# Whole attention products and an uneven second layer in a fused attention and feed-forward kernel

## The chip, the cores and the metric

The kernel runs on one core of one Trainium2 chip. The core has a matrix engine (TensorE, PE in the profile, with its weight loads shown apart as PEld), a vector engine (VectorE, DVE), an activation engine (ScalarE, ACT), GpSimd (POOL) and SyncE (SP), which issues transfers here. Matrix results go to PSUM, an accumulator memory that the kernel divides into eight banks of 512 float32 columns on 128 partitions. The metric is the device time of one execution in microseconds (us); lower is better. Times of a single instruction are in nanoseconds (ns) where marked.

## The reference

The input is a batch of 8 with 8 heads, 576 tokens and 64 features for each head. Attention keeps only scores within `tau` of the row's maximum; its output, with the heads side by side, is the input of a two-layer block with a hard-swish gate.

```python
def _attn_ref(q, k, v, tau):                       # (8, 8, 576, 64)
    scale = 1.0 / np.sqrt(q.shape[-1])
    scores = scale * np.matmul(q, k.transpose(0, 1, 3, 2))
    thresh = np.max(scores, axis=-1, keepdims=True) - tau
    scores = np.where(scores >= thresh, scores, -1000000000.0)
    scores = scores - np.max(scores, axis=-1, keepdims=True)
    attn = np.exp(scores)
    attn = attn / (np.sum(attn, axis=-1, keepdims=True) + 1e-09)
    return np.matmul(attn, v).astype(np.float32)

def _moe_ref(x, w_in, w_out):                      # x (4608, 512)
    h = x @ w_in                                   # first layer, 512 -> 2048
    relu6 = np.clip(h + 3.0, 0.0, 6.0)
    g = h * relu6 / 6.0
    return (g @ w_out).astype(np.float32)          # second layer, 2048 -> 512
```

## The kernel before

Four heads of one batch are a quad; there are 16. A quad has nine slots: slots 0 to 3 are the four blocks of 128 queries of the first pair of heads, 4 to 7 those of the second pair, and slot 8 holds the last 64 queries of all four heads. The main loop runs over all 144 slots, `n`. From slot `N1 = 22` on it works in periods of two slots: scores of two slots are computed together at the end of an odd slot.

In each slot the loop weaves together softmax work for some slots, a piece of the first layer (`mm1`, eight matmuls of 256 columns or four of 512), attention products of a quad that is done (`multiply`), and, in even slots, half an output tile of the second layer (`second`, 8 of its 16 matmuls). The order of the statements is the order of the instructions on each engine.

```python
HB, OB = 6, 7                        # PSUM banks of the first and second layer

def bank():                          # banks 2 and 5 in turn: products, transposed last keys
    nonlocal turn
    turn += 1
    return ps[:, (2, 5)[turn % 2], :]

def first(n):
    return n > N1 + 2 and n % 2

def score_col(n, a):                 # scores of odd slots end inside banks 2 and 5
    return (704 if first(n) else 128) + (0 if a else 1536)

def scores(n):
    quad, slot = divmod(n, NSLOT)
    w0 = 320 if first(n) else 384
    for k0, w in ((0, w0), (w0, S - w0)):
        ...                          # two heads side by side, float32, 64 rows each
```

An attention product takes 128 probabilities by 64 values at a time. The two heads of a pair lie in the two halves of the output's partitions. `av_main` does the 512 queries of a pair (or part of them, by `c0` and `w`), `av_rest` the last 64 of four heads:

```python
def av(pb, pair, pT, cols):
    b, hp = divmod(pair, NPAIR)
    vm, vr = vsb[b]
    for c in range(4):
        for a in range(2):
            nc.tensor.matmul(pb[a * 64:(a + 1) * 64, :], vm[:, 2 * hp + a, c * D:(c + 1) * D],
                             pT[:, 5 * a + c, cols], start=(c == 0), stop=False)
    for a in range(2):
        nc.tensor.matmul(pb[a * 64:(a + 1) * 64, :], vr[:, a, hp, :], pT[:, 4, cols], start=False, stop=True)

def av_main(pair, c0=0, w=512):
    ...
    pb = bank()[:, 0:w]
    av(pb, pair, pts[pair], slice(c0, c0 + w))
    return lambda: nc.vector.tensor_copy(out=xT[b][:, hp, c0:c0 + w], in_=pb)
```

Which product follows which slot (counted from the quad's first) is in a table. In quads 2 to 15 each pair is done in two halves of 256 queries, in every second slot:

```python
if quad < NB:                        # NB = 2
    jobs = ((8, p0, 0, 512), (12, p1, 0, 512), (13, None, 0, 0))
else:
    jobs = [(7 - quad % 2 + 2 * i, *of) for i, of in enumerate(
        ((p0, 0, 256), (p0, 256, 256), (p1, 0, 256), (p1, 256, 256), (None, 0, 0)))]
```

The part of the loop that sets the order (cut):

```python
        if n + 1 < len(queue):
            sm_max(queue[n + 1])              # VectorE: scores out of PSUM, with the row's maximum
        even = n >= N1 and n % 2 == 0
        if n > N1:
            sm_recip(prev)
        for copy in waiting:                  # output of a second-layer tile, query transposes
            copy()
        waiting = []
        if todo1:
            item, then = todo1.pop(0)
            ...
            h = mm1(item, 0 if n == len(queue) - 1 else OB if n > N1 and n % 2 and not pieces else HB)
        if n >= N1:
            for copy in multiply(n):          # products, and their copies out of PSUM (VectorE)
                copy()
        if item:
            mm1_gate(item, h, mm1_relu(h, on_act=even))   # ReLU: ScalarE in even slots, else VectorE
        ...
            second()                          # 8 second-layer matmuls, in even slots
        if n >= N1:
            for i in range(2):
                sm_exp(sl, i)                 # ScalarE
            if n + 1 < len(queue):
                for i in range(2):
                    sm_mask(queue[n + 1], i)  # ScalarE
        ...                                   # transposes of later queries and keys
        elif n % 2:
            for m in (n + 3, n + 2):          # the even slot's scores first
                if m < len(queue):
                    scores(m)
        if n > 0:
            sm_norm(prev)                     # GpSimd, then a transposing transfer
```

Of the kernel before, what the change touches and what calls it, by code (L numbers as in the profile page):

```python
# [15 lines left out]
P = 128  # L16
# [4 lines left out]
def kernel(  # L21
# [11 lines left out]
    B, H, S, D = q.shape  # L33
# [4 lines left out]
    NI = d_ff // P  # L38
# [320 lines left out]
    def av_rest(quad):  # L359
        b, g = divmod(quad, 2)  # L360
        pb = bank()
        for n in range(2):
            av(pb[:, n * 64:(n + 1) * 64], 2 * quad + n, ptr[quad], slice(n * 64, (n + 1) * 64))
        if b % 2 == 0 and g == 0:
            xR[b // 2] = x_pool.tile([P, KI, P], BF16, tag="xR", name="xR")
        o0 = 64 * (b % 2)
        return lambda: nc.vector.tensor_copy(out=xR[b // 2][:, 2 * g:2 * g + 2, o0:o0 + 64],
                                             in_=pb[:, 0:P].rearrange("p (a b) -> p a b", a=2))
# [42 lines left out]
    def mm2_part(bb, mt, part, ob=OB):  # L411
        if part == 0:
            o_ps[0] = ps[:, ob, :]
        for ni in range(part * 4, part * 4 + 4):
            nc.tensor.matmul(o_ps[0], gbuf[:, ni, mt * P:(mt + 1) * P], w_out_sb[:, ni, :],  # L415
                             start=(ni == 0), stop=(ni == NI - 1))
# [23 lines left out]
    def moe_of(b):  # L440
        items = []
        for c0, mts in (((0, (5, 6)), (None, (4,)), (256, (7, 8))) if b % 2 else ((0, (0, 1)), (256, (2, 3)))):
            for ni in range(0, NI, 4 if c0 is None else 2):
                items.append(((b, ni, c0), ()))
            items[-1] = (items[-1][0], [(b // 2, mt, part) for mt in mts for part in range(4)])
# [41 lines left out]
    for quad in range(1, NQUAD):  # L487
        n0 = quad * NSLOT
        first_odd = n0 - 9 + quad % 2
        for i, (job, of) in enumerate((("q", 2 * quad), ("k", 2 * quad), ("rest", quad),  # L490
                                       ("q", 2 * quad + 1), ("k", 2 * quad + 1))):
            turn_at(n0 + (-5, -4, -3, 0, 1)[i] if quad < 3 else
                    first_odd + (0, 2, 3, 4, 6)[i] if quad > 3 else first_odd + (0, 2, 3, 5, 7)[i], job, of)

    products = {}
    for quad in range(NQUAD):
        p0, p1 = 2 * quad, 2 * quad + 1
        if quad < NB:
            jobs = ((8, p0, 0, 512), (12, p1, 0, 512), (13, None, 0, 0))
        else:  # L500
            jobs = [(7 - quad % 2 + 2 * i, *of) for i, of in enumerate(
                ((p0, 0, 256), (p0, 256, 256), (p1, 0, 256), (p1, 256, 256), (None, 0, 0)))]
# [3 lines left out]
    def multiply(n):  # L506
        copies = []
        for of, pair, *columns in products.get(n, ()):
            copies.append(av_rest(of) if pair is None else av_main(pair, *columns))
# [5 lines left out]

    def second():
        nonlocal pieces, bb, mt, part
        pieces = 2 if now % 2 == 0 and todo2 else 0
        for _ in range(pieces):
            bb, mt, part = todo2.pop(0)  # L520
            mm2_part(bb, mt, part)
# [3 lines left out]
    pieces = bb = mt = part = 0  # L525
    waiting = []
    for n, sl in enumerate(queue):
# [23 lines left out]
        for copy in waiting:  # L551
            copy()
        waiting = []

        if todo1:
# [3 lines left out]
            h = mm1(item, 0 if n == len(queue) - 1 else OB if n > N1 and n % 2 and not pieces else HB)  # L559
# [3 lines left out]
        if n >= N1:  # L563
            for copy in multiply(n):
                copy()
        if item:
            mm1_gate(item, h, mm1_relu(h, on_act=even))
        copies = pe_transpose(queue[n - 2]) if n > 1 and queue[n - 2].on_chip else None
# [20 lines left out]
        if part == 3:  # L589
            waiting.append(lambda tile=(bb, mt): late.extend(mm2_out(*tile, on_act=False)))  # L590
            part = 0
# [37 lines left out]
    count = [1, 0 if todo2 and todo2[0][2] else 1]  # L629
# [16 lines left out]
    def rest2():  # L646
        while todo2:
            bb, mt, part = todo2.pop(0)
            mm2_part(bb, mt, part, ob=OB - count[1] % 2)
            if part == 3:  # L650
                flush()
                if (bb, mt) == (B // 2 - 1, 8):
                    last_out()
                else:
                    late.extend(mm2_out(bb, mt, on_act=(count[1] % 2 == 0)))
                count[1] += 1

    av_main(2 * last + 1, 0, 256)()
    for item in todo1:
        rest1(*item, on_act=False)  # L660
# [48 lines left out]
```

## Time and profile before

| what | value |
|---|---|
| time, median of three runs | 520.26 us (520.13 to 520.81) |
| span of the profiled execution | 518.3 us |
| granted clock of TensorE, mean | 0.999 |
| costliest TensorE lines, busy | scores L287 174.0 us, second layer L415 134.1 us, first layer L381 130.9 us, products L346 39.1 us |
| costliest VectorE line | maximum L302, 205.1 us |
| costliest ScalarE lines | mask L309 205.8 us, exponential L314 192.5 us |

The profile's page gives for each engine the busy time, its share of the span and the number of instructions. Groups of instructions carry the line of the kernel, the engine, the operation, the tiles (output, arrow, inputs), the count, and then the busy time and the mean time of one. The timeline merges neighbouring instructions of one kind: start in us from the span's beginning, time from the first start to the last end, engine, line, operation, and in brackets how long the engine had been idle and what ended that. The ends of matmuls are modelled; the time from the start of one group to the start of the next is the measure of TensorE's work. The chain of waits follows the execution back from its last instruction, at each step to what released it.

### The profile page before, as it was taken

How to read it: one execution, taken by the hardware profiler on the slowest of the kernel's cores; microseconds unless marked ns; L12 is line 12 of the kernel's file. 1: busy time of each engine (PE TensorE's matmuls, PEld its weight loads, DVE VectorE, ACT ScalarE, POOL GpSimd, SP SyncE). 2: the span in 40 equal slices, each digit the busy share in tenths (PEclk: the TensorE clock that was granted, in tenths of full speed). 3: DMA queues.
4: the chain of work that ended last, by engine and by line, in shares of the span. 5: the costliest groups of instructions: out<-in, count | busy, mean ns of one | idle time of the engine just before them, and what ended most of it. 6: DMA issues, size and time to landing. Idle time of an engine off the chain costs nothing.

```text
span 518.3 us, 12124 instructions
## 1 busy us (share of the span) xinstructions
PE 505.9 (98%) x4145; PEld 321.1 (62%) x4145; DVE 442.6 (85%) x1124; ACT 452.1 (87%) x980; POOL 299.3 (58%) x538
## 2 busy tenths in 40 slices
PE   8999999999999999999999999999999999999997
PEld 6765556666665666666665666666665666667563
DVE  3788887998999999999999999999999999887261
ACT  3999979999999999999999999999999999987060
POOL 1778869756676666657566656657566655552000
PEclk9999999999999999999999999999999999999999
DMA  5899899989999999999979998999999997564222
GB/s 132 123 173 163 142 161 156 174 147 171 167 178 157 170 162 183 177 170 179 177 150 164 157 199 159 166 166 178 167 163 168 178 178 123 114 113 71 77 67 61
DMA packets 314094, 78.77 MB, mean 152 GB/s; under 512 B 296624, under 2 KB 309168, under 8 KB 314032
## 3 DMA queue, kind: packets, MB, share of 16 engines
q1 hardware_dynamic: 294464, 67.90, 76.0%
q0 software_dynamic: 18368, 9.71, 15.1%
q8 instruction: 32, 0.52, 0.4%
q10 hardware_dynamic: 1200, 0.39, 0.3%
q14 instruction: 30, 0.25, 0.2%
HBM read 36.70 MB, written 9.44 MB: 89 GB/s over the span
## 4 chain that ended last, share of the span: by engine, by line
PE 81%; ACT 3%; DVE 2%; POOL 0%; issue 0%; POOLq 0%
PE ps L287 25%; PE ps L415 24%; PE ps L381 21%; PE ps L346 7%; PE ps L376 3%; ACT s L314 1%; PE ps L349 1%; ACT s L309 1%; DVE g L404 1%; ACT r L389 1%; DVE s L302 0%; DVE r L391 0%; POOL pn L322 0%; PE ps L257 0%; ACT kT L222 0%; DVE xT L357 0%
## 5 line engine op out<-in xcount | busy, mean ns | idle before, releaser
L322 POOL TENSOR_SCALAR pn<-s,rinv 128x576 bf16<-128x576 f32 x288 | 210.6, 743 | 19.0 <-issue 4.5
L302 DVE TENSOR_SCALAR_CACHE_REDUCE s<-ps 128x576 f32<-128x576 f32 x288 | 205.1, 749 | 17.6 <-PE ps L287 9.0
L309 ACT ACTIVATE s<-s,bias 128x576 f32<-128x576 f32 x288 | 205.8, 763 | 6.0 <-POOL bias L305 5.7
L314 ACT ACTIVATE s<-s 128x576 f32<-128x576 f32 x288 | 192.5, 671 | 0.3
L287 PE MATMUL ps<-kT,qT 64*128 64x384 f32 (+7 forms) x1280 | 174.0, 419 | 4.7 <-DVE s L302 3.8
L287 PEld LDWEIGHTS ps<-kT,qT 64*128 64x128 f32 (+1 forms) x1280 | 103.6, 175 | 59.3 <-issue 15.8
L415 PE MATMUL ps<-w_out_sb,g 128*128 128x512 bf16 x576 | 134.1, 379 | 0.0
L381 PE MATMUL ps<-xT,w_in_sb 128*128 128x256 bf16 x1024 | 130.9, 273 | 0.2 <-DVE g L404 0.2
L381 PEld LDWEIGHTS <-w_in_sb 128*128 128x128 bf16 x1024 | 95.5, 98 | 40.0 <-issue 20.8
L305 POOL TENSOR_SCALAR bias<-m 128x2 f32<-128x2 f32 x144 | 26.9, 187 | 154.5 <-DVE rinv L317 136.6
L404 DVE SCALAR_TENSOR_TENSOR g<-r,ps 128x512 bf16<-128x512 f32 x128 | 87.9, 687 | 15.2 <-ACT r L389 11.2
L415 PEld LDWEIGHTS <-g 128*128 128x128 bf16 x576 | 56.2, 98 | 56.8 <-issue 0.4
L389 ACT ACTIVATE r<-ps,three 128x512 f32<-128x512 f32 x81 | 55.6, 687 | 27.9 <-PE ps L381 23.8
L314 ACT ACTIVATION_READ_ACCUMULATOR s<-s 128x1 f32 x288 | 54.5, 189 | 0.0
L391 DVE TENSOR_SCALAR r<-ps 128x512 f32<-128x512 f32 x63 | 42.9, 681 | 0.0
L346 PE MATMUL ps<-pT,vm 128*64 128x256 bf16 (+1 forms) x480 | 39.1, 285 | 0.0
L346 PEld LDWEIGHTS <-vm 128*64 128x64 bf16 x736 | 27.3, 110 | 16.0 <-issue 14.3
L357 DVE CAST xT<-ps 128x256 bf16<-128x256 f32 (+1 forms) x60 | 26.3, 438 | 11.8 <-PE ps L349 11.8
L423 DVE TENSOR_SCALAR osb<-ps 128x512 f32<-128x512 f32 x31 | 20.9, 673 | 8.4 <-PE ps L415 8.4
L302 DVE DVE_READ_ACCUMULATOR s<-ps 128x1 f32 x288 | 23.9, 83 | 0.0
L317 DVE RECIPROCAL rinv<-rsum 128x2 f32<-128x2 f32 x144 | 23.0, 160 | 0.6 <-ACT s L314 0.6
L143 POOL DMA_DIRECT2D vm<-in_v_dram x28 | 21.4, 765 | 0.7 <-issue 0.7
(57 smaller groups left out, 259.4 us busy)
## 6 DMA issues: line engine op xcount, KB each, us to landing
out_dram<-osb SPq DMA_DIRECT2D x31, 256.0 KB, 2.9
nq<-in_q_dram SPq DMA_DIRECT2D x96, 72.0 KB, 3.5
km<-in_k_dram SPq DMA_DIRECT2D x96, 64.0 KB, 3.2
vm<-in_v_dram POOLq DMA_DIRECT2D x24, 128.0 KB, 4.0
km<-in_k_dram SPq DMA_DIRECT2D x16, 128.0 KB, 3.6
w_in_sb<-in_moe_w_in_dram POOLq DMA_DIRECT2D x16, 128.0 KB, 3.6
w_out_sb<-in_moe_w_out_dram POOLq DMA_DIRECT2D x16, 128.0 KB, 4.1
pT<-pn SPq DMA_TRANSPOSE x117, 4.0
```

The source lines that it names most:

```text
L287: nc.tensor.matmul(ps_flat[rows, c0:c0 + w], qT_of(pair)[a * 64:(a + 1) * 64, q0:q0 + rows.stop - rows.start], kT_of(pair)[a * 64:(a + 1) ...
L302: nc.vector.tensor_scalar(out=sl.s[:, i, :], in0=ps_flat[:, c0:c0 + S], scalar1=1.0, scalar2=None, op0=Alu.mult, op1=Alu.max, accum_out=sl ...
L305: nc.gpsimd.tensor_scalar(out=sl.bias[:], in0=sl.m[:], scalar1=-scale, scalar2=tau, op0=Alu.mult, op1=Alu.add)
L309: nc.scalar.activation(out=s, in_=s, func=Act.Prelu, bias=sl.bias[:, i:i + 1], scale=scale, alpha=REJECT)
L314: nc.scalar.activation(out=s, in_=s, func=Act.Exp, accum_out=sl.rsum[:, i:i + 1])
L322: nc.gpsimd.tensor_scalar(out=pn[:, i, :], in0=sl.s[:, i, :], scalar1=sl.rinv[:, i:i + 1], scalar2=1.0, op0=Alu.mult, op1=Alu.mult)
L346: nc.tensor.matmul(pb[a * 64:(a + 1) * 64, :], vm[:, 2 * hp + a, c * D:(c + 1) * D], pT[:, 5 * a + c, cols], start=(c == 0), stop=False)
L381: nc.tensor.matmul(ps[:, hb, n * 256:(n + 1) * 256], w_in_sb[:, ki, (ni + n) * P:(ni + n + 1) * P], xT[b][:, ki, c0:c0 + 256], start=(ki = ...
L389: nc.scalar.activation(out=r, in_=hps, func=Act.Relu, bias=three[:])
L391: nc.vector.tensor_scalar(out=r, in0=hps, scalar1=3.0, scalar2=0.0, op0=Alu.add, op1=Alu.max)
L404: nc.vector.scalar_tensor_tensor(out=out, in0=r, scalar=6.0, in1=hps, op0=Alu.min, op1=Alu.mult)
L415: nc.tensor.matmul(o_ps[0], gbuf[:, ni, mt * P:(mt + 1) * P], w_out_sb[:, ni, :], start=(ni == 0), stop=(ni == NI - 1))
```

## The change

Most attention products of quads 2 to 15 are done whole, in 512 columns, where they were done in two halves; in quads 3, 7, 11 and 15 the second pair stays in halves. That makes the matmul work of products uneven among periods: some have 512 or more columns, some none. To even it out, the 16 second-layer matmuls of a token tile are no longer split 8 and 8 over the tile's two periods, but by the products near them: 5 and 11, 7 and 9 and so on. After a short part, the first-layer block of the odd slot goes to the bank of `bank()` that was used last (2 or 5) and not to `HB`, which the gate of the even slot may still read, and a product of the last 64 queries in that slot takes `HB`. The copies of products and the output of a second-layer tile stand behind the ReLU and the gate on VectorE, where they stood ahead. In even quads from 4 on, the transposition of the last keys (`"rest"`) comes two slots sooner. The product of the last 64 queries of a quad comes two slots sooner.

```diff
-    def av_rest(quad):
+    def av_rest(quad, pb=None):
         b, g = divmod(quad, 2)
-        pb = bank()
+        pb = bank() if pb is None else pb
...
-    def mm2_part(bb, mt, part, ob=OB):
-        if part == 0:
+    def mm2_part(bb, mt, n0, n1, ob=OB):
+        if n0 == 0:
             o_ps[0] = ps[:, ob, :]
-        for ni in range(part * 4, part * 4 + 4):
+        for ni in range(n0, n1):
...
-                    first_odd + (0, 2, 3, 4, 6)[i] if quad > 3 else first_odd + (0, 2, 3, 5, 7)[i], job, of)
+                    first_odd + (0, 2, 3 if quad % 2 else 1, 4, 6)[i] if quad > 3 else first_odd + (0, 2, 3, 5, 7)[i], job, of)
...
-            jobs = [(7 - quad % 2 + 2 * i, *of) for i, of in enumerate(
-                ((p0, 0, 256), (p0, 256, 256), (p1, 0, 256), (p1, 256, 256), (None, 0, 0)))]
+            jobs = (((9, p0, 0, 512), (13, p1, 0, 512), (13, None, 0, 0)) if quad % 2 == 0 else
+                    ((8, p0, 0, 512), (10, p1, 0, 256), (12, p1, 256, 256), (12, None, 0, 0)) if quad % 4 == 3 else
+                    ((8, p0, 0, 512), (12, p1, 0, 512), (12, None, 0, 0)))
...
-    def multiply(n):
+    def multiply(n, apart=False):
...
-            copies.append(av_rest(of) if pair is None else av_main(pair, *columns))
+            copies.append(av_rest(of, ps[:, HB, :] if apart else None) if pair is None else av_main(pair, *columns))
...
+    def columns_at(n):
+        return sum(of[3] or P for of in products.get(n, ()))
+
     def second():
-        nonlocal pieces, bb, mt, part
-        pieces = 2 if now % 2 == 0 and todo2 else 0
-        for _ in range(pieces):
-            bb, mt, part = todo2.pop(0)
-            mm2_part(bb, mt, part)
+        nonlocal pieces, done
+        pieces = 0
+        if now % 2 == 0 and todo2:
+            pieces = NI - done if done else NI // 2 + round((columns_at(now + 3) - columns_at(now + 1)) / 200)
+            mm2_part(*todo2[0], done, done + pieces)
+            done += pieces
...
-        for copy in waiting:
-            copy()
-        waiting = []
+        if n <= N1:
+            for copy in waiting:
+                copy()
+            waiting = []
...
-            h = mm1(item, 0 if n == len(queue) - 1 else OB if n > N1 and n % 2 and not pieces else HB)
+            apart = n > N1 and n % 2 and 0 < pieces < NI // 2
+            h = mm1(item, 0 if n == len(queue) - 1 else OB if n > N1 and n % 2 and not pieces else
+                    (2, 5)[turn % 2] if apart else HB)
...
-        if n >= N1:
-            for copy in multiply(n):
-                copy()
+        copies = multiply(n, item and apart) if n >= N1 else []
         if item:
             mm1_gate(item, h, mm1_relu(h, on_act=even))
+        if n >= N1:
+            for copy in copies + waiting:
+                copy()
+            waiting = []
```

Left out above is the bookkeeping of tiles and of the code behind the loop, which does the same work in the same order, except that it finds a tile with 9 of its 16 matmuls still to do (8 before) and one whole product in the place of a half.

## The prediction

> **What bounds the kernel now.** I read the page's first two parts, then the table of stretches, then the timeline and the chain of waits of one stretch in the middle. The page says which engine is full:
>
> ```profile
> PE 505.9 (98%) x4145; PEld 321.1 (62%) x4145; DVE 442.6 (85%) x1124; ACT 452.1 (87%) x980; POOL 299.3 (58%) x538
> ...
> 240.00:280.00 40.00, 40.00 (x330) 25.09 (x329) 38.14 (x99) 38.13 (x84) 24.14 (x44) 1.00 0.94 169
> ```
>
> 98% of TensorE (PE) alone proves little, since the ends of matmuls are modelled. In the second line, of the stretches, VectorE (DVE) and ScalarE (ACT) are also busy for 38.1 of 40 us: nearly as full. The timeline shows what paces them. One period is two slots; its TensorE part (start, duration of the group, line of the kernel):
>
> ```profile
> 260.37 0.63 PE L346 MATMUL ps<-pT,vm 128*64 128x256 bf16 x8
> 260.83 0.28 PE L349 MATMUL ps<-pT,vr 128*64 128x256 bf16 x2
> 261.04 2.21 PE L287 MATMUL ps<-kT,qT 64*128 64x384 f32 x16
> 263.18 1.05 PE L381 MATMUL ps<-xT,w_in_sb 128*128 128x256 bf16 x8
> 264.07 1.89 PE L415 MATMUL ps<-w_out_sb,g 128*128 128x512 bf16 x8
> 265.79 1.04 PE L381 MATMUL ps<-xT,w_in_sb 128*128 128x256 bf16 x8
> 266.76 0.63 PE L346 MATMUL ps<-pT,vm 128*64 128x256 bf16 x8
> 267.22 0.28 PE L349 MATMUL ps<-pT,vr 128*64 128x256 bf16 x2
> 267.43 2.21 PE L287 MATMUL ps<-kT,qT 64*128 64x384 f32 x16
> ```
>
> From start to start the costs are: scores 2.14, first layer 0.88 or 0.89, second layer 1.72 or 1.73 for eight matmuls, first layer 0.97, half an attention product 0.67; together 6.39 us, without a hole. The chain of waits for 254.4 to 280.3 names TensorE lines only. So TensorE sets the pace here, and its time from start to start is what counts. ScalarE and VectorE have this room in the same period:
>
> ```profile
> 264.27 0.69 ACT L389 ACTIVATE r<-ps,three 128x512 f32<-128x512 f32 x1 [0.31 <-PE ps L381]
> ...
> 261.15 0.42 DVE L357 CAST xT<-ps 128x256 bf16<-128x256 f32 x1 [0.36 <-PE ps L349]
> ...
> 264.99 0.69 DVE L404 SCALAR_TENSOR_TENSOR g<-r,ps 128x512 bf16<-128x512 f32 x1
> ...
> 266.94 0.16 DVE L317 RECIPROCAL rinv<-rsum 128x2 f32<-128x2 f32 x1
> 267.02 0.67 DVE L423 TENSOR_SCALAR osb<-ps 128x512 f32<-128x512 f32 x1
> ```
>
> ScalarE waits 0.3 us for the first layer, VectorE 0.36 us for the attention product. The second maximum ends at about 266.94, which is 5.90 after the scores began at 261.04, so VectorE releases the next scores about 0.4 us before TensorE comes for them. Before 105 us it is different: scores there take up to 2.9 us in the chain of waits, and the chain runs through ScalarE's masks and exponentials. I expect nothing from the change there.
>
> [...]
>
> **The change part by part.** The steady pattern repeats after four quads, 18 periods, 196.16 to 312.63 us by the scores' starts: 116.47 us.
>
> (1) Whole products. In 18 periods there are now 16 half products and four rests of 64 columns. Fourteen halves stand alone at 0.67 (9.38), two follow a rest (0.34 + 0.65 each, 1.98), two rests stand alone at 0.44 (0.88): 12.24 us. Afterwards there are seven whole products, two halves (the last pair of every fourth quad stays split) and four rests. A whole product was measured in the early stage at 1.20 from start to start; four alone are 4.80, three with a rest behind (1.20 + 0.33) 4.59, a half 0.67, a half with a rest 0.99: 11.05. Saved: 1.19 us, nearly all of it drains. Nine of 18 periods then have no product and go from first layer straight to scores; at 77.80 to 78.80 that step was 1.00, against 0.97 before a product, which gives 9 x 0.02 to 0.03, about 0.2, back.
>
> (2) The uneven split moves 3 of 16 second-layer matmuls, 3 x 0.216 = 0.65 us, from periods with a whole product into those without. It adds no work. Period with product: 2.14 + 0.88 + 5 x 0.216 + 0.97 + 1.20 = 6.27. Without: 2.14 + 0.88 + 11 x 0.216 + 0.99 = 6.39. With product and rest: 6.60. In two neighbours of every 18 no product is near either period of the tile, so the split is 8/8 and TensorE needs only 5.84 and 5.89.
>
> (3) The other bank for the first-layer block behind a short part removes a wait on the gate of the block before: in the four periods with a slot 8 the second layer took 1.82 before it instead of 1.73, up to 4 x 0.09 = 0.36 back.
>
> (4) The copies of products now stand behind ReLU and gate on VectorE. It no longer waits 0.36 for the product, and saves 7 x (838 - 690) = about 1 us in 18 periods, but the bank of the product comes free later.
>
> (5) Last keys of even quads, two slots sooner: the same 0.11 us on TensorE and the same two copies on ScalarE, moved to a period without product. No sum of its own.
>
> TensorE alone: -1.19 + 0.2 - 0.2 (half of the 0.36) = -1.2 of 116.47, 1.0%.
>
> **What it gives back.** VectorE's loop has a floor: scores 2.14, first layer 0.88, its end to ReLU 0.2, ReLU on ScalarE 0.7, gate 0.6, maximum 1.36, release 0.1: 6.0 us. The periods with 5.84 and 5.89 cannot be that short. The first follows the heaviest VectorE tail: maximum and reciprocal end at about 6.02, then ReLU 0.71, gate 0.60, copy 0.61, rest 0.20, output 0.59, key transpose 0.63 to 9.36, which is 2.76 into a period whose TensorE part before was 6.60. The maximum should start at 2.33, so all is 0.4 later, and the floor becomes 6.3; the second also holds the 24 score matmuls (2.30), floor 6.16. Lost: 0.48 + 0.27 = 0.75. And the copy of a whole product: reciprocal done at 5.98, + 0.71 + 0.60 + 0.69 = 7.98, or 1.71 into the next period, while the second half of the odd slot's scores wants that bank at 1.6. That is 0.1 to 0.15 in the three or four periods of 6.27 or 6.43: 0.3 to 0.5. Lost together 1.05 to 1.25. So the working leaves -0.1 to +0.1 in 18 periods, near nothing.
>
> **Rivals.** First, TensorE's saving arrives whole because VectorE's pieces overlap better than my steps: the freed wait of 0.36 in each product period speaks for it, VectorE's 95% share of the stretch against it. The steady part from 105.6 to 461.6 is 356 us, 3.06 patterns; x 1.2 = 3.7 us, so 516.6. Second, VectorE takes over as the pace: heavy periods sum to 4 x 0.67 + 0.16 + 0.60 + 1.31 + 0.61 + 0.20 + 0.59 + 0.69 = 6.84 against TensorE's 6.60. For it speaks the copy's late release; against it that the neighbours need only 5.3 and take up what is late. If each whole product stalls 0.4, 7 x 0.4 - 1.2 = +1.6 in 18 periods, 4.9 us, so 525. Third, ScalarE: in a period it does eight masks and exponentials at 0.66 from start to start and a ReLU of 0.58, 5.9 us, with the keys' copies (0.54) 6.44; in a period of 6.3 it has little room, but the wait of 0.3 absorbs it: nothing. Transfers: probabilities of the rest land 4.4 us (median) after issue, and are wanted one period (6.4 us) sooner than now; I count some 3 us of room (normalised until about 5.5 us into a period, landed at 10, read near 12.5 in odd quads).
>
> **Range and chances.** Between the working, 520, and the full saving, 516.6, I take 518.8, 0.3% under the time before, because my stalls on VectorE are upper estimates: I added its steps with no overlap. The range reaches from the saving with a little from the first stage, 515.0, to 0.3% slower, 521.8. Over 2% faster would need 10 us, nearly three times all that TensorE saves: 0.03. Over 2% slower needs 0.6 us lost in each product period: 0.03.
>
> **What would show it.** Right: product groups of 512 columns at 1.20 from start to start and about 24 drains fewer; periods with product at 6.3 to 6.4 and those without at about 6.4; the two light periods at 6.0 to 6.3 with TensorE waiting for VectorE's maximum or copy. The waits would hold new lines, TensorE scores behind the product's copy (the cast) and behind the maximum, some 1 us in 18 periods. Wrong: no such waits, and 18 periods at about 115.2 (the first rival), or waits of 0.4 us at every whole product (the second). A wait for a transfer of probabilities, or ScalarE at the end of the chain, would mean that I missed the cause altogether.

## The result and the profile after

The changed kernel takes 526.04 us (median of three runs, 525.09 to 527.6) against 520.26 before: a ratio of 1.011, with a 95% interval of 1.0072 to 1.0153. It is 1.1% slower, and the time lies above the whole predicted range. The profiled execution has a span of 525.8 us, 7.5 more than before. From the page after, the busy times, the granted clock and the chain of waits by engine and by line, and below it the chain by engine from the page before:

```profile
PE 506.4 (96%) x3862; PEld 316.3 (60%) x3905; DVE 442.1 (84%) x1100; ACT 452.3 (86%) x980; POOL 299.3 (57%) x538
...
PEclk9999998999999999999999999999999999999999
...
PE 72%; ACT 8%; DVE 3%; DMA 2%; issue 1%; POOL 0%; SPq 0%; DVEq 0%; POOLq 0%
PE ps L287 23%; PE ps L415 21%; PE ps L381 19%; PE ps L346 5%; ACT s L314 3%; ACT s L309 3%; PE ps L376 3%; DMA pR<-pn 2%; ACT r L389 2%; DVE g L404 1%; PE ps L349 1%; DVE r L391 1%; DVE s L302 1%; DVE xT L357 0%; ACT kT L222 0%
```

```profile
PE 81%; ACT 3%; DVE 2%; POOL 0%; issue 0%; POOLq 0%
```

TensorE's busy time is as before (506.4 against 505.9) although it has fewer instructions; some matmul records are missing (the page has 540 of 576 for the second layer), and busy ends are modelled, so this sum says little. The other two lines say more. The granted clock has one 8 where every slice was 9, and the chain of waits, which was 81% TensorE and 3% ScalarE, is 72% and 8% now; a transfer of probabilities (`pR<-pn`) has come into it, where no transfer stood before. So the loss is not one of TensorE's work.

Cut at the starts of the same groups of scores, the two traces differ by stage as follows (us):

| stage | before | after | more | of that |
|---|---|---|---|---|
| up to 79 | 78.80 | 79.19 | 0.4 | within the spread of all profiled executions, 78.64 to 79.80 |
| next four periods | 26.77 | 28.64 | 1.9 | clock 1.1, VectorE's order 0.7 (below) |
| 15 periods | 97.24 | 98.68 | 1.4 | one wait for a transfer, 1.4 |
| 18 periods, the prediction's pattern | 116.46 | 116.97 | 0.5 | one wait for a transfer, 0.2 |
| 22 periods | 142.35 | 144.44 | 2.1 | one wait for a transfer, 1.4 |
| tail, without scores | 56.64 | 57.91 | 1.3 | one wait for an output copy, 1.0 |

**The steady part.** The first line below is the stretch from 240 to 280 us, which had TensorE, VectorE and ScalarE at 40.00, 38.14 and 38.13 before. The others are TensorE's timeline for one period with a whole product and the next without one:

```profile
240.00:280.00 40.00, 39.74 (x303) 24.37 (x308) 37.12 (x93) 37.66 (x85) 24.93 (x46) 1.00 0.97 165
```

```profile
265.41 2.21 PE L287 MATMUL ps<-kT,qT 64*128 64x384 f32 x16
...
268.44 1.24 PE L415 MATMUL ps<-w_out_sb,g 128*128 128x512 bf16 x5
...
270.48 1.05 PE L346 MATMUL ps<-pT,vm 128*64 128x512 bf16 x8
...
271.68 2.46 PE L287 MATMUL ps<-kT,qT 64*128 64x384 f32 x16
274.08 1.04 PE L376 MATMUL ps<-w_in_sb,xR 128*128 128x512 bf16 x3
274.95 2.54 PE L415 MATMUL ps<-w_out_sb,g 128*128 128x512 bf16 x11
...
278.39 0.92 PE L287 MATMUL ps<-kT,qT 64*128 64x384 f32 x4
```

From start to start the first period is 6.27 (265.41 to 271.68), with the product at 1.20. The next is 6.71: it has the expected 11 second-layer matmuls at 2.37, but its scores take 2.39 (to the first-layer group, of which one record is missing) instead of 2.14. VectorE's timeline, and below it that of TensorE's weight loads, show what they wait for:

```profile
271.39 0.67 DVE L391 TENSOR_SCALAR r<-ps 128x512 f32<-128x512 f32 x1
272.10 0.69 DVE L404 SCALAR_TENSOR_TENSOR g<-r,ps 128x512 bf16<-128x512 f32 x1
272.70 0.68 DVE L357 CAST xT<-ps 128x512 bf16<-128x512 f32 x1
```

```profile
273.44 0.30 PEld L287 LDWEIGHTS ps<-kT,qT 64*128 64x128 f32 x4 [0.49 <-DVE xT L357]
```

The copy of the product ends at 273.38, 1.70 us into the period, and until then the product's bank is not free for the second half of the odd slot's scores.

**The light periods.** In the two neighbours without a product, ScalarE is what ends last. ScalarE's timeline, and TensorE's behind it:

```profile
314.46 0.69 ACT L389 ACTIVATE r<-ps,three 128x512 f32<-128x512 f32 x1 [0.80 <-PE ps L381]
...
321.05 0.69 ACT L389 ACTIVATE r<-ps,three 128x512 f32<-128x512 f32 x1
```

```profile
322.51 1.03 PE L381 MATMUL ps<-xT,w_in_sb 128*128 128x256 bf16 x8 [0.16 <-DVE g L404]
```

From the start of one ReLU (L389) to that of the next it has no idle time: the ReLU, four exponentials, four masks and the copies of keys fill 6.59 us. The first-layer block waits for the gate, the gate for this ReLU, and the chain of waits runs along ScalarE from 314.46 to 321.75. It does so at each of the three places with two light periods behind 105 us.

**The early stage.** TensorE's timeline from 84 to 92 us, and below it the stretches of 1 us each, with TensorE's busy time, the granted clock, the DMA share and GB/s:

```profile
86.38 4.15 PE L287 MATMUL ps<-kT,qT 64*128 64x384 f32 x16 [1.68 <-DVE s L302]
90.46 1.42 PE L381 MATMUL ps<-xT,w_in_sb 128*128 128x256 bf16 x8
```

```profile
86.00:87.00 1.00, 0.62 (x2) 1.00 1.34 208
87.00:88.00 1.00, 1.00 (x8) 0.92 1.29 206
88.00:89.00 1.00, 1.00 (x5) 0.50 1.82 294
89.00:90.00 1.00, 1.00 (x6) 0.50 0.69 47
90.00:91.00 1.00, 1.00 (x6) 0.50 1.06 170
91.00:92.00 1.00, 0.98 (x8) 0.88 1.32 167
```

The kernel before has this line in the same place of its timeline, and a clock of 1.00 throughout:

```profile
85.99 2.88 PE L287 MATMUL ps<-kT,qT 64*128 64x384 f32 x16 [1.00 <-DVE s L302]
```

Before, half a product of quad 2 (slot 25) filled part of TensorE's wait for the maximum. It is gone, the hole grew from 1.00 to 1.68 us, and shortly after it the clock was 0.50 for about 3.4 us. The scores took 4.08 instead of 2.81.

**The transfer.** TensorE's timeline in quad 5, then the normalising by GpSimd (POOL) and the issuing queue (SPq) before it:

```profile
191.30 1.05 PE L346 MATMUL ps<-pT,vm 128*64 128x512 bf16 x8
192.19 0.38 PE L349 MATMUL ps<-pT,vr 128*64 128x512 bf16 x2
193.83 0.32 PE L346 MATMUL ps<-pR,vm 128*64 128x64 bf16 x8 [1.26 <-DMA pR<-pn]
```

```profile
186.22 1.47 POOL L322 TENSOR_SCALAR pn<-s,rinv 128x576 bf16<-128x576 f32 x2
```

```profile
186.68 1.36 SPq L330 DMA_TRANSPOSE pT<-pn  x1
188.14 0.56 SPq L436 DMA_DIRECT2D out_dram<-osb  x1
188.80 1.42 SPq L330 DMA_TRANSPOSE pR<-pn  x1
```

GpSimd and the queue keep the order of the slots, so the probabilities of the last 64 queries are those normalised from 186.22 to 187.69. The queue is then still busy with the slot before and with an output, and issues at 188.80 the transfer for which the product waits. TensorE goes on 5.0 us after the issue.

**The tail.** The last second-layer part behind the scores, in TensorE's timeline:

```profile
467.92 1.20 PE L287 MATMUL ps<-kT,qT 64*64 64x320 f32 x16
470.09 1.67 PE L415 MATMUL ps<-w_out_sb,g 128*128 128x512 bf16 x7 [0.97 <-DVE osb L423]
```

And before:

```profile
461.62 1.25 PE L287 MATMUL ps<-kT,qT 64*64 64x320 f32 x16
462.80 1.90 PE L415 MATMUL ps<-w_out_sb,g 128*128 128x512 bf16 x8
```

It is 2.17 us from the last scores to the second layer; before it was 1.18. The output copy of that slot now stands behind a ReLU and a gate.

### The profile page after: what moved, and what is told of

It reads as the page before. It is cut to its first block, busy times and chain, and to the rows that moved or that the text cites. A ratio compares the mean times of both kernels' runs of the same rounds, so it can differ in the third digit from the quotient of the medians.

```text
span 525.8 us, 11627 instructions
## 1 busy us (share of the span) xinstructions
PE 506.4 (96%) x3862; PEld 316.3 (60%) x3905; DVE 442.1 (84%) x1100; ACT 452.3 (86%) x980; POOL 299.3 (57%) x538
## 4 chain that ended last, share of the span: by engine, by line
PE 72%; ACT 8%; DVE 3%; DMA 2%; issue 1%; POOL 0%; SPq 0%; DVEq 0%; POOLq 0%
PE ps L287 23%; PE ps L415 21%; PE ps L381 19%; PE ps L346 5%; ACT s L314 3%; ACT s L309 3%; PE ps L376 3%; DMA pR<-pn 2%; ACT r L389 2%; DVE g L404 1%; PE ps L349 1%; DVE r L391 1%; DVE s L302 1%; DVE xT L357 0%; ACT kT L222 0%
## 5 line engine op out<-in xcount | busy, mean ns | idle before, releaser
L287 PE MATMUL ps<-kT,qT 64*128 64x384 f32 (+7 forms) x1280 | 179.5, 422 | 4.9 <-DVE s L302 3.6
L287 PEld LDWEIGHTS ps<-kT,qT 64*128 64x128 f32 (+1 forms) x1280 | 107.8, 176 | 63.7 <-DVE s L302 11.5
L415 PE MATMUL ps<-w_out_sb,g 128*128 128x512 bf16 x540 | 130.1, 379 | 2.9 <-DVE osb L423 1.0
L389 ACT ACTIVATE r<-ps,three 128x512 f32<-128x512 f32 x81 | 55.6, 687 | 34.7 <-PE ps L381 28.3
L346 PE MATMUL ps<-pT,vm 128*64 128x512 bf16 (+1 forms) x288 | 34.5, 361 | 0.0
L346 PEld LDWEIGHTS <-vm 128*64 128x64 bf16 x544 | 20.0, 110 | 19.0 <-issue 7.1
L357 DVE CAST xT<-ps 128x512 bf16<-128x512 f32 (+1 forms) x36 | 22.4, 625 | 1.4 <-PE ps L349 1.4
```

The source lines that it names most:

```text
L287: nc.tensor.matmul(ps_flat[rows, c0:c0 + w], qT_of(pair)[a * 64:(a + 1) * 64, q0:q0 + rows.stop - rows.start], kT_of(pair)[a * 64:(a + 1) ...
L389: nc.scalar.activation(out=r, in_=hps, func=Act.Relu, bias=three[:])
```

## The experiments

All ratios are to the kernel before. Edits are to the changed kernel, unless it says otherwise. Where two are compared by stages, the stages are those of the table above.

**The three places of the loss.** First the rest of the odd quads 1, 5, 9 and 13 two slots later, where it was before:

```diff
-                    ((8, p0, 0, 512), (12, p1, 0, 512), (12, None, 0, 0)))
+                    ((8, p0, 0, 512), (12, p1, 0, 512), (14, None, 0, 0)))
```

> The changed kernel with one edit: in quads 1, 5, 9 and 13 the product of the last 64 queries follows slot 14 (as before the change) and not slot 12. Theory (the matmuls waited for the transposing transfer of the last queries' probabilities, 1.3 us in each of two periods and 0.2 in a third): no wait of a product on that transfer is left, and the time falls by about 2.9 us, from 526.0 to about 523. Rival (the wait only takes up slack that VectorE lacks there anyway, so it comes back as a wait for VectorE in the next period): the transfer's wait goes, but the time stays at 525 to 526.

531.52 us, 1.0211 (1.0185 to 1.0236). A miss, and by the edit's own doing. The waits for the transfer were gone, but the moved rest counts as 128 columns in the split and changed it in its neighbourhood, so the first-layer block counted as one "behind a short part" and went to bank 2 or 5, where last keys were still being copied. The waits of this kernel, engine and line with total, times and longest:

```profile
PE ps L381 <- ACT kT L222: 6.7, 3, 2.2
```

Behind two of these three waits, holes of 2.23 us, the clock fell to 0.50 as well. What follows: the transfer's wait and the banks are tied through the split. Next, the waiting copies early again:

```diff
-        if n <= N1:
+        if n <= N1 + 1 or n == len(queue) - 1:
```

> The changed kernel with one edit: in slot 23 and in the last slot the waiting copies (a query transpose out of PSUM, and the output of a second-layer tile) stand ahead of ReLU and gate on VectorE again, as before the change. Theory: the late query copy held up the scores at 86 us (that period took 8.2 us for 6.0), and the late output held the second layer's bank after the last scores (1.0 us), so the time falls by 1.9 + 1.0 = 2.9 us to about 523. Rival (the stage before 105 us is paced by ScalarE, so an earlier copy gives nothing there): only the 1.0 us at the end, to about 525.

525.87 us, 1.0105 (1.0077 to 1.0133). The edit named slots in which nothing waits, so the kernel has the changed kernel's instructions one for one: it is a repeat. As that it is useful. The early stage (28.64, clock 0.50 for 3.4 us) and the tail (57.89) came out alike; the waits for the transfer were 0.6, 0.4 and none, instead of 1.4, 0.2 and 1.4. They vary from one execution to the next.

Both edits together:

> Both edits of the two runs before together. If the two causes are independent, their gains add: 526.0 - 2.9 - 2.9 = about 520.2, that is the time of the kernel before within 0.3%, and what is left of the change gains nothing, since waits of the scores for the copy of a whole product (0.25 us each, some five in 18 periods) eat what TensorE saves. If whole products were a gain that these two causes hid, the time would be 517 or less. If other waits of the new order matter more, it stays above 522.

532.95 us, 1.023 (1.0201 to 1.026): the first edit again, since the second did nothing. Then the two repaired. For the copies, the slots that have something waiting (25, and the third from the end):

```diff
-        if n <= N1:
+        if n in (N1 + 3, len(queue) - 3) or n <= N1:
```

> The changed kernel with one edit: in slots 25 and 141 the waiting copies (the second query transpose of quad 3, and one output of the second layer) stand ahead of ReLU and gate on VectorE, as before the change. Theory: the late query copy held bank 2 or 5 and with it the second half of the odd slot's scores at 88 us (0.7 us), and the late output held the second layer's bank behind the last scores (1.0 us); both waits go, and the time falls by 1.7 us to about 524.3. TensorE's granted clock still drops to a half for 3.4 us at 88 us, because its cause, the gap of 1.7 us ahead of these scores, stays. Rival (both waits hide others that end at the same time): within 0.5 us of 526.

524.04 us, 1.0064 (1.0049 to 1.0079). The tail is at 56.88 again, which is 1.0 of the loss. The clock still fell early, and the stage is no shorter (28.71 for 28.64), so of the 0.7 us that I expected from the early copy of queries nothing is seen. What else the profiled execution gains lies in the waits for the transfer, which were shorter in it. For the rest, slot 14 as in the first run, and a rest by itself no longer counted in the split:

```diff
-        return sum(of[3] or P for of in products.get(n, ()))
+        of = products.get(n, ())
+        return sum(job[3] or P for job in of) if any(job[3] for job in of) else 0
```

> The changed kernel with the last queries' product of quads 5, 9 and 13 behind slot 14 again, and a product of last queries alone not counted in the split of the second layer (so the first-layer block there stays in its own bank). Theory: no wait of a product for the transposing transfer is left (0.9 to 2.9 us in the two traces of the changed program), and nothing takes its place: 523.5 to 525. Rival (the wait only covered VectorE's lag): the wait for the transfer goes, but waits for VectorE grow by as much, 526.

523.9 us, 1.0067 (1.005 to 1.0084). No wait for the transfer is left. The mean granted clock of its four executions is 0.998, 1.0, 0.996 and 0.996; in all seven of the changed kernel and its repeat it is 0.996 or 0.997, so part of the 2.1 us by which the median lies under the changed kernel's is the clock. The two at 0.996 took 524.16 and 524.63, some 1.4 to 1.9 less than the changed kernel. In the profiled execution the clock stayed up, with the same instructions in this stage. TensorE's timeline:

```profile
86.17 2.45 PE L287 MATMUL ps<-kT,qT 64*128 64x384 f32 x12 [1.67 <-DVE s L302]
88.84 0.70 PE L287 MATMUL ps<-kT,qT 64*128 64x256 f32 x4 [0.22 <-DVE qT L239]
```

The hole is the same, 1.67, and the scores take 3.31; the stage is 27.50 against 28.64. So the lower clock costs 1.1 us when it comes, and 0.7 is lost without it. Part of that is the second line: the last scores wait 0.22 for a bank until the copy of queries (L239), which now stands behind ReLU and gate, is done. Then the half product back into the hole, with quad 2's first pair in halves:

```diff
-            jobs = (((9, p0, 0, 512), (13, p1, 0, 512), (13, None, 0, 0)) if quad % 2 == 0 else
+            jobs = (((7, p0, 0, 256), (9, p0, 256, 256), (13, p1, 0, 512), (13, None, 0, 0)) if quad == 2 else
+                    ((9, p0, 0, 512), (13, p1, 0, 512), (13, None, 0, 0)) if quad % 2 == 0 else
```

> The changed kernel with the first pair of quad 2 alone in halves, behind slots 25 and 27, as before the change. Theory (leaving the product out of slot 25 made a gap of 1.7 us on TensorE, and the gap made the granted clock fall to a half for 3.4 us, which cost some 1.1 us): the gap is 1.0 us or less, the clock stays at 1.0 until the end, and the time falls by 1.1 to 1.9 us, to 524.1 to 524.9. Rival (the clock's drop is hidden behind ScalarE, which paces this stage): the clock stays up, but the time does not fall by more than 0.4 us.

525.61 us, 1.0091 (1.0074 to 1.0109). In the trace the hole is 1.01 again, the clock stays at 1.00 and the stage is 27.69; and the mean clock is 0.999 or 1.0 in all four executions. But the median lies only 0.4 below the changed kernel's, less than I expected and less than the executions of either differ. One thing goes that way: the copy of queries now holds the scores longer (0.55). The stage is 0.95 shorter all the same; why the median does not show it stays open. All three repairs together:

> The changed kernel with the three edits together: waiting copies early in slots 25 and 141, last queries' product behind slot 14 in quads 5, 9 and 13, first pair of quad 2 in halves. If the three causes are independent their measured gains add: 526.0 - 2.0 - 2.1 - 0.4 = 521.5, and TensorE's clock stays at 1.0 until the end. What is left above the time before is then the steady part, 18 periods at about 116.7 for 116.5, with waits of the scores for the copy of a whole product of some 0.25 us in each of five or more periods. Rival (whole products gain once the rest is mended): 519 or less.

522.4 us, 1.0035 (1.0022 to 1.0048). Of the 5.8 us lost (526.04 less 520.26), 3.6 come back; 0.35% remains. In the early stage the repair is not complete (27.68 against 26.77 before): the copy of queries is early, but now the scores wait just as long for the copy of the half product, which stands behind the gate.

```profile
88.83 0.70 PE L287 MATMUL ps<-kT,qT 64*128 64x256 f32 x2 [0.55 <-DVE xT L357]
```

**Which parts are needed.** VectorE's old order everywhere, with all else of the change:

```diff
-        if n <= N1:
-            for copy in waiting:
-                copy()
-            waiting = []
+        for copy in waiting:
+            copy()
+        waiting = []
...
+        for copy in copies:
+            copy()
...
-        if n >= N1:
-            for copy in copies + waiting:
-                copy()
-            waiting = []
```

> The changed kernel with VectorE's old order: copies of products and all waiting copies ahead of ReLU and gate, in every slot; whole products, uneven split and earlier last keys stay. Theory (the new order causes the late query copy and the late output, 2.9 us, but is needed for whole products, because a copy that stands ahead makes VectorE wait some 0.5 us for each product's end): waits of VectorE's copy for the product come back (about 0.4 us each, some 24 times), the scores' waits for the copy go, and the time is 523 to 527. Rival (the new order is the fault altogether): about 520 or less with the transfer's wait of 2.9 us still in, so 520 to 523, and no loss on VectorE.

536.78 us, 1.0309 (1.0273 to 1.0345), a miss. The scores now wait for the gate:

```profile
PEld ps L287 <- DVE g L404: 17.1, 24, 1.1
...
PE ps L287 <- DVE g L404: 5.8, 13, 0.6
```

Behind a short part the first-layer block lies in bank 2 or 5, so its gate releases a bank that the scores want, and with the copies ahead of it the gate becomes the later release. With this bank the change needs the new order. That a whole product needs it in itself is not shown: in the kernel with the product first, below, the block is back in `HB`, the copy stands ahead of the gate, and the scores never wait for it. The early stage is 26.87 here, though its hole is 1.67 (the clock stayed up): without the new order 0.1 is lost there. The reverse, the new order with products in halves and the split 8/8 (and so the block in `HB`; the earlier keys stay):

```diff
-            jobs = (((9, p0, 0, 512), (13, p1, 0, 512), (13, None, 0, 0)) if quad % 2 == 0 else
-                    ((8, p0, 0, 512), (10, p1, 0, 256), (12, p1, 256, 256), (12, None, 0, 0)) if quad % 4 == 3 else
-                    ((8, p0, 0, 512), (12, p1, 0, 512), (12, None, 0, 0)))
+            jobs = [(7 - quad % 2 + 2 * i, *of) for i, of in enumerate(
+                ((p0, 0, 256), (p0, 256, 256), (p1, 0, 256), (p1, 256, 256), (None, 0, 0)))]
...
-            pieces = NI - done if done else NI // 2 + round((columns_at(now + 3) - columns_at(now + 1)) / 200)
+            pieces = NI - done if done else NI // 2
```

> The changed kernel with products in halves behind the slots of before, and the second layer split 8 and 8: what is left of the change is VectorE's new order and the earlier last keys. Theory (the new order costs only where a copy was late at 88 us and at the end): 520.3 + 0.7 + 1.0 = about 522, 18 periods at 116.5 as before, clock at 1.0 throughout, since the half product fills the gap ahead of the scores at 86 us. Rival 1 (the new order itself costs in each period): 524 or more, with 18 periods over 117. Rival 2 (the order is free, whole products are the fault): 520.3.

521.88 us, 1.0028 (1.0015 to 1.0041). The 18 periods take 116.44, as before. The order by itself costs nothing there; its cost is at the two ends, 1.2 in the early stage (27.97) and 0.7 in the tail (57.33).

The even split, in the kernel with the three repairs:

```diff
-            pieces = NI - done if done else NI // 2 + round((columns_at(now + 3) - columns_at(now + 1)) / 200)
+            pieces = NI - done if done else NI // 2
```

> As the run with the three edits, but with the second layer split 8 and 8 throughout. Theory (the uneven split only makes room on TensorE that waits for VectorE then take): periods with a whole product need 2.14 + 0.88 + 1.73 + 0.97 + 1.20 = 6.92 and have no wait of the scores for the copy, those without one are held up by VectorE's loop at 6.0 to 6.1; a pair is 12.9 to 13.0, as now (6.27 + 6.70), and with a rest 13.25 to 13.35 for 13.0: 0 to 1 us more in 18 periods, so 521.5 to 524.5. Rival (the split carries the saving): a pair costs 0.65 more, eight in 18 periods, 5 us, so 537.

528.92 us, 1.0161 (1.0148 to 1.0174), more than expected. The 18 periods take 118.87 against 116.69. TensorE's timeline, from the light period at 213.60 on:

```profile
213.60 2.21 PE L287 MATMUL ps<-kT,qT 64*128 64x384 f32 x16
...
219.43 2.42 PE L287 MATMUL ps<-kT,qT 64*128 64x384 f32 x16
221.78 1.05 PE L381 MATMUL ps<-xT,w_in_sb 128*128 128x256 bf16 x8
...
224.88 1.03 PE L381 MATMUL ps<-xT,w_in_sb 128*128 128x256 bf16 x8 [0.32 <-DVE g L404]
...
227.36 2.21 PE L287 MATMUL ps<-kT,qT 64*128 64x384 f32 x16
```

A light period of 5.83 is followed by one of 7.93, where the first layer waits for the gate and the scores take 2.35. What is behind after the short one is ScalarE: again 6.59 from ReLU to ReLU (216.83 to 223.42), and the chain of waits runs along it from there through this ReLU and the gate to the first layer at 224.88. ScalarE has 15% of this kernel's chain, against 3% before. The pair is 13.76; with the uneven split it is 13.31 (6.72 and 6.59). The edit also takes away the other bank, which only a short part gives, and the nine waits of the first layer for the gate (2.5 us in all, none in the repaired kernel) are for `HB`. So split and bank together are worth 2.2 us in 18 periods, though they add and save no work; what each is worth, this run does not tell.

The last keys two slots later again, also in the repaired kernel:

```diff
-                    first_odd + (0, 2, 3 if quad % 2 else 1, 4, 6)[i] if quad > 3 else first_odd + (0, 2, 3, 5, 7)[i], job, of)
+                    first_odd + (0, 2, 3, 4, 6)[i] if quad > 3 else first_odd + (0, 2, 3, 5, 7)[i], job, of)
```

> As the run with the three edits (522.4 us), but the last keys of even quads are transposed two slots later again, as before the change. They then fall into periods with a whole product, where the first-layer block goes to the bank of the last keys. Theory (the earlier keys are what keeps that bank free): in two periods of 18 the block waits for ScalarE's copy of the keys, 1 to 2.5 us each as in the run where the last queries' product met them, 2 to 5 us in 18 periods, so 528 to 537. Rival (the keys' place is indifferent, as the prediction had it): 522 to 523.

541.28 us, 1.0403 (1.0384 to 1.0421), beyond what I expected. The waits name the cause, the first layer behind ScalarE's copy of keys in the bank that it is given:

```profile
PE ps L381 <- ACT kT L222: 16.0, 6, 2.7
```

Six waits, as many as there are even quads from 4 to 14, make 16 of the 18.9 us by which it is above the repaired kernel; behind two of them the clock fell to 0.50 for about 3.4 us. The earlier keys are what makes the other bank free.

**Can the saving arrive?** In the repaired kernel, the copies in the old order in all periods without a product:

```diff
-        if n <= N1:
+        if n <= N1 + 3 or not products.get(n):
```

> As the run with the three edits, but in every slot without a product the waiting copies (output of the second layer, transposed queries) stand ahead of ReLU and gate, where VectorE waits 0.5 us for the first-layer block anyway. Theory: VectorE is late by up to 0.5 us less in the periods after an output without a product, the scores' start of 2.5 us in two periods of 18 goes back to 2.3; 0.3 to 0.6 us in 18 periods, 1 to 2 us in all: 519.5 to 520.5. Rival (lateness is made good in the next period anyway): 521 to 521.5.

521.88 us, 1.0031 (1.0019 to 1.0043). The 18 periods are unchanged, 116.69: the waits lie behind the product and not in the other slots. So in the next kernel, on top of this edit, the product stands ahead of the odd slot's first-layer block, and its copy ahead of the ReLU, both a microsecond sooner (core of the edit):

```diff
-            apart = n > N1 and n % 2 and 0 < pieces < NI // 2
-            h = mm1(item, ... (2, 5)[turn % 2] if apart else HB)
+            copies = multiply(n) if n > N1 else []
+            h = mm1(item, 0 if n == len(queue) - 1 else OB if n > N1 and n % 2 and not pieces else HB)
...
+        for copy in copies:
+            copy()
```

> As the run with waiting copies in the gap, but in odd slots the attention product stands ahead of the first-layer block on TensorE, and its copy ahead of ReLU and gate on VectorE; the first-layer block stays in its own bank. Theory (the scores wait for banks 2 and 5, which the copy of the product and the gate release too late): the product ends 1 us sooner, its copy is done about 0.4 us into the next period, no wait of the scores for a copy or gate is left; one more drain of 0.1 us in each of nine periods with a product is paid for it: 18 periods go from 116.6 to about 116.1, the time to 518 to 519.5, under the kernel before. Rival (the drains cost as much as the waits, or VectorE is the pace anyway): 520 to 522.

520.86 us (520.24 to 525.49 in 21 runs), 1.0025 (1.001 to 1.0041). The bank's wait is gone, as TensorE's timeline of the two periods shown above has it:

```profile
261.60 2.21 PE L287 MATMUL ps<-kT,qT 64*128 64x384 f32 x16
...
264.63 1.24 PE L415 MATMUL ps<-w_out_sb,g 128*128 128x512 bf16 x5
265.80 1.05 PE L346 MATMUL ps<-pT,vm 128*64 128x512 bf16 x8
...
267.00 1.05 PE L381 MATMUL ps<-xT,w_in_sb 128*128 128x256 bf16 x8
267.98 2.21 PE L287 MATMUL ps<-kT,qT 64*128 64x384 f32 x16
270.12 1.04 PE L376 MATMUL ps<-w_in_sb,xR 128*128 128x512 bf16 x4
```

The scores at 267.98 take 2.14. But the first period is 6.38 instead of 6.27: before the product, which has another tiling (128*64 for 128*128), five second-layer matmuls take 1.17 and not 1.08, and this, the drain that I had expected, gives back some 0.1 for each product; and one wait for a transfer of whole blocks took 1.0 us, so the 18 periods came to 117.57. Without that they would be 116.6, no better than before. Seven of the 21 executions took 522.65 or more; the profiled one, 521.4, is not among them, so what slows those is not shown. Last, product first, except where the product of the last 64 queries follows late:

```diff
+            ahead = n > N1 and not any(of % 4 == 1 and pair == 2 * of + 1 for of, pair, *_ in products.get(n, ()))
+            copies = multiply(n) if ahead else None
```

> As the run with the product ahead of the first-layer block (520.9 us), but in slot 12 of quads 5, 9 and 13 the product stands behind that block again. Theory (what is left there is a wait for the transfer of the last probabilities of a pair, which comes and goes from one execution to the next): no product waits for a transfer, the executions lie close together, 18 periods at 116.4 to 116.6, time 520.0 to 520.6, the same as the kernel before, since the nine drains of 0.1 us added and the ones saved cancel. Rival (TensorE's saving of 1.2 us in 18 periods arrives once the transfer is out of the way): 517.5 or less.

522.39 us, 1.0041 (1.0025 to 1.0057), 18 periods 116.98. A miss; this version also put the waiting outputs ahead of the ReLU in product slots, so it does not say which of the two undid the gain. No version that I ran is faster than the kernel before.

## Why the prediction was wrong

**TensorE's work (steps 1 to 3): right.** The products of 18 periods take 10.98 us where I had 11.05, a period with product 6.27 and with a rest 6.59, as worked out. If I add up all groups of the 18 periods at their shortest, TensorE needs 114.96 us; the same sum for before is 116.24, and 0.2 of its 116.46 are small waits. So about 1.3 is saved in work and 0.2 in waits, 1.5 against "-1.2 of 116.47". Of "nearly all of it drains" the runs show only times: a whole product takes 1.20 where two halves took 1.34, and seven times that difference is 0.98 of the 1.19. What TensorE does in that time they do not show.

**What it gives back: right in kind, too small.** Three times the scores behind a whole product wait 0.25 for its copy, not "0.1 to 0.15". The end of the copy I had at 1.71 into the period, and it is at 1.70: the wrong term was when the scores want the bank. In a period without the wait the last four weight loads of the scores would start 1.5 after the first (16 in 1.81, the last four 0.30), and not "at 1.6"; here they started at 1.76. With two smaller ones that makes 0.86 where I had "0.3 to 0.5"; the two light periods lose 0.53 and the one behind them 0.39, together 0.92 against "0.48 + 0.27 = 0.75", and not where I had put it: the first ran at 5.83, unheld, and the second at 6.41. (For the first, my own 6.0 and 0.4 make 6.4 and not 6.3.) The floor was that of another engine, too: the second is held by ScalarE and not by VectorE's loop. Given back: 1.8 instead of "1.05 to 1.25". So the 18 periods end 0.3 above before, without the transfer's 0.2; the working had said -0.1 to +0.1. Had the rest of the kernel behaved so, I would have been inside the range.

**"I count some 3 us of room": failed.** I took the transfer as landed 10 us after its period's start. TensorE could go on at 14.2 (193.83, with the period's start at 179.61), and wanted to at about 12.8. The term that I mis-sized most is the end of the normalising: 8.1 (187.69), not "about 5.5", which is the slot before it (184.01 to about 185.5). The place in the issue queue added 1.1, which I had not counted, and the landing took some 5.0 where I had 4.4, the median of 3.2 to 6.8 before. In the profiled execution this costs 3.0 us; the run with the rest two slots later, not counted in the split, takes it away, and its median is 2.1 under the changed kernel's, a part of which is the clock. I had named such a wait as the sign that I missed the cause.

**"I expect nothing from the change there": failed.** The stage before 105 us loses 1.9: 1.1 through the clock (28.64 against 27.50, same instructions) and 0.7 through VectorE's new order, which keeps a bank from the scores. The order alone costs 1.2 (27.97); with the old order the stage is 26.87 (the run with the order back), and with product and copy first 26.96. The copy of queries is not the whole of it: with that early, the copy of the product takes its place. That the hole lowers the clock is shown by the run that fills it (1.01 us): no execution under 0.999, where all seven of the changed kernel and its repeat were at 0.996 or 0.997. It does not do so each time: of the seven profiled executions with this hole the clock fell in four and stayed up in three.

**Step 4 left out the other copies.** I spoke of the products' copies alone; the output and the queries wait in the same list. At the end this is 1.0 us, shown by the run with copies early. The step's 838 and 690 ns are two copies of 256 columns at 419 and one of 512 at 690, the means in the profile before; in the one after they are 418 and 685.

**Step 5, "No sum of its own": wrong in its meaning.** The keys' time is indeed moved and not added, but without it the kernel loses 18.9 us: it is what the other bank rests on.

**The rivals.** The full saving did not come. VectorE as the pace, at 525, has nearly the right number for a wrong reason: it asked for 0.4 at every whole product, and the 18 periods show 0.3 net, not 1.6. ScalarE, to which I gave "nothing", costs some 0.5 in 18 periods: with the copies of keys I had it at 6.44, and the second light period, in which the chain of waits runs along it, took 6.41.

## What to carry to other kernels

Before work is taken out of a stage, look at what it covered there: half a product in a wait for another engine was free, and its removal lengthened the hole by 0.68 us, as much as it takes (0.67). A sum over the steady pattern does not bound a change of order; go through the first and last slots, and through every other thing that stands in the list that is moved. When a consumer is moved earlier, count its transfer from the moment at which the queue can issue it, not from when its data are ready (1.1 us sooner here), and when periods are made uneven, compare the shortest with what every other engine needs in it.

## What was not expected of the hardware

The granted clock fell to 0.50 for about 3.4 us after TensorE had been idle for 1.68 us. It did not fall after each such hole. In the profiled executions it fell after four of seven holes of 1.67 or 1.68 us, four of six of 2.23 or 2.24 (the first experiment and that with both edits), and two of six of about 2.67 (the run with the keys back). After the two holes of 1.26 us in the loop of the changed kernel, after those of 1.3 and 1.4 in the run with quad 2's first pair in halves, that with the three edits and that with the product first (mean clock 1.0 in each), and after those of about 1.0, it stayed up. What decides after which hole it falls is not shown.

Where the next group had another tiling, a group of matmuls took longer: eight of the first layer 0.88 or 0.89 before the second layer and 0.97 before a product, in the kernel before. The product put first makes it visible: five second-layer matmuls take 1.08 before a first-layer block (268.44 to 269.52 in the changed kernel) and 1.17 before a product (264.63 to 265.80), some 0.1 for each switch. The drains of the prediction and of the expectations are this time; what takes it is not shown.
